# Linear attention with two channel mixes on one core: running sums ahead of the second tile's loads, last outputs in two column parts, fillers in planned TensorE gaps

## The chip, the cores and the metric

The kernel runs on one core of a Trainium2 chip. The metric is the device time of one execution in microseconds. Three timed executions of the kernel before took 407.04, 409.69 and 410.55 us, median 409.69. The profiled execution took 407.03 us; its profile spans 405.2 us, so 1.8 us lie outside the span.

## The reference, cut to what matters

```python
# attention: 4 batches x 8 heads, 768 steps, head size 32, state 16, in chunks
cum = np.cumsum(log_a_of_the_chunk)                  # running sums
L = np.exp(cum[:, None] - cum[None, :]) * causal
y = ((C @ B.T) * L) @ x  +  (C @ state) * np.exp(cum)
state = np.exp(sum(log_a)) * state + (B * decay_from_j).T @ x
# channel mix on the 3072 rows of 256 (x_prev is x one step earlier)
xk = mu_k * x + (1 - mu_k) * x_prev ; xr = mu_r * x + (1 - mu_r) * x_prev
k = np.maximum(xk @ w_k, 0)                          # 256 -> 1024
x = sigmoid(xr @ w_r) * ((k * k) @ w_v)              # w_r 256 -> 256, w_v 1024 -> 256
# second mix
h = np.maximum(np.maximum(x @ w1, x @ w2), x @ w3)   # 256 -> 768
out = h @ w_out                                      # 768 -> 256
```

The activations come as float32 and the weights as float64.

## The kernel before, in words

The 3072 rows are worked through in six tiles of 512 (t = 0 to 5). Each tile goes through attention, the gate (w_r, `gate`, matmuls on line L986), the first mix (`ffn`: eight blocks f of w_k on L1011, then w_v on L1032), `combine`, the maxout over w1, w2 and w3 (`maxout`, L689), and the projection by w_out (`project`, L1108, evacuated on L1079 by ScalarE and L1081 by VectorE).

To keep float32 precision every operand of the large products is split into a high and a low part (names that end in h and l), and each product is three matmuls: high x high, high x low, low x high. The high part is a copy (L414, mostly ScalarE), the low part a subtraction (L422, VectorE or GpSimd).

The float64 weights are fetched as pairs of 32-bit words into a buffer h (for w_k also woh) and made into float32 by five steps: ScalarE L630, then VectorE L631, L633, L635 and L637. After that they are split like the rest. In the order listings h_94 and h_93 are the two large fetch buffers, h_92 and wd or wol hold the words being converted. The first block of w_k for each of the two row halves (w_k0, into h, and w_k1, into woh) serves f = 0 to 3; the second half of w_k (into h_93, then wol, with low part wkl) serves f = 4 to 7.

Attention of tile 0: spreads (L703, L704) make the exponents of L, L860 the scores C times B, L872 on VectorE the product with L, L773 gathers the states (block c = 0 or 1), L895 multiplies by x, L885 adds what the state carries, and the copy L933 writes the result xb in two halves, one on ScalarE and one on VectorE. L966 and L968 mix it with the row before into tmp, which is split into k2h and k2l for the gate of tile 0. The running sums over the sequence (L600, L611; evacuated by L604 and by L605, an Exp) go out to DRAM as crd and ced and come back for the later tiles. For tile 1 the spread is on L719, L721 and L727; L727 is a burst of small matmuls.

All loads and stores are issued by SyncE in program order. The order of every engine's instructions is written by a planner, the class `Plan`: it simulates all operations with estimated durations, repeats the simulation with new priorities for `ROUNDS` times, and issues the operations by the start times of the best round. `first=` and `bias` shift priorities, `FETCH`, `HEAVY` and `OPEN` are its guesses for instruction fetch and DMA, `AHEAD` shifts the mix of tile 0 and the w_k conversions. Loads of tile 1 and the second half of w_k may not be issued before the operation in `begun['loads']` has ended; before the change that is L848, the product ce of tile 0. `Plan.issue` also puts a filler matmul (128x512, bfloat16) into a gap of the planned TensorE timeline if the gap is long enough, up to a time `stop`, the first planned start of a gate's matmul. `idle`, the end of the last TensorE operation there, is computed from its start and its estimated cost.

Of the kernel before, what the change touches and what calls it, by code (L numbers as in the profile page):

```python
# [11 lines left out]
AF = mybir.ActivationFunctionType  # L12
# [63 lines left out]
class Plan:  # L76
# [14 lines left out]
    FIRST = 1500.0  # L91
    STAY = 8000.0
    BLOCK, FRONT = 128, 92
    FETCH = ((9000.0, 5600.0), (16500.0, 2800.0), (30000.0, 5000.0), (60000.0, 3200.0), (1e9, 2600.0))
    OPEN = (1000.0, 28.0)
    HEAVY = (2100.0, 16000.0, 1300.0)
    WARM = (3400.0, 430.0, 215.0, 100.0, 600.0)
    EARLY = 104
    ROUNDS = 60
    SPARE = (200.0, 1000.0)  # L100
# [213 lines left out]
    def issue(self):  # L314
        ops, start, where = self.ops, self.start, self.where
        idle = 0.0
        stop = min(start[i] for i in self.wait_for)
        for i in sorted(range(len(ops)), key=lambda k: (start[k], k)):
            fn = ops[i][1]
            if where[i] == "PE":  # L320
                for _ in range(0 if idle else self.EARLY):
                    self.narrow()
                if self.WARM[0] < start[i] < stop:
                    gap = start[i] - max(idle, self.WARM[0]) - self.WARM[3 + (idle > 0.0)]
                    for _ in range(0 if start[self.switch[0]] < start[i] <= start[self.switch[1]] else int(gap / (self.WARM[1] if start[i] < self.COLD else self.WARM[2]))):
                        self.filler(idle > 0.0)
                idle = start[i] + ops[i][0]["PE"]
            if where[i]:
                fn(where[i]) if len(ops[i][0]) > 1 else fn()

# [6 lines left out]
SPREAD = 2  # L337
LATE = 0
EARLY1 = -20000.0
AHEAD = (60000.0, 60000.0)  # L340
FIRST = (9.85e5, 9.8e5, 9.9e5, 9.83e5, 9.5e5, 9.95e5, 9.6e5)


# [1 line left out]
def kernel(  # L345
# [56 lines left out]
    def act(n):  # L402
        return 93 + 0.833 * n

    def tt(n):
        return 68 + 1.042 * n
# [18 lines left out]
    def dma(cost, out_, in_, r=(), w=(), first=0.0, **k):  # L425
        plan.bias += first
        i = op("SP", 0.8 * cost, lambda: Q.dma_start(ap(out_), in_), r=r, w=w, **k)
        plan.bias -= first
        return i
# [167 lines left out]
    def sums():  # L597
        b_er.readers = [op("DVE", 130, lambda: V.tensor_copy(tri_r, tri_f), r=[b_cr], w=[b_tri], after=[begun['spread']])]
        p = boot.bufs[3]
        op("PE", 350, lambda p=p: [T.matmul(  # L600
            p.ap[:QH, s * P:(s + 1) * P], la[:, s * QH:(s + 1) * QH], tri, start=True, stop=True) for s in range(2)],
            r=[b_la, b_tri], w=[p])
        pr = p.ap[:QH, :2 * P].rearrange("r (s x) -> r s x", s=2)
        op("ACT", act(256), lambda: A.activation(crow[:, :, 0], pr, AF.Copy), r=[p], w=[b_cr])  # L604
        op("ACT", act(256), lambda: A.activation(crow[:, :, 1], pr, AF.Exp), r=[p], w=[b_er])  # L605
        for s in range(2):
            dma(200, ced[s * QH:(s + 1) * QH], crow[:, s, 1], r=[b_er], w=[b_ced[s]])
            dma(200, crd[:, s * QH:(s + 1) * QH].rearrange("c q i -> q c i"),
                crow[:, s, 0].rearrange("q (c i) -> q c i", c=2), r=[b_cr], w=[b_crd[s]], first=EARLY1)
        p = boot.bufs[2]  # L610
        op("PE", 350, lambda p=p: T.matmul(p.ap[:, :NC], tri, la, start=True, stop=True), r=[b_la, b_tri], w=[p])  # L611
        b_cc.readers = [k for s in (b_af, b_ts) for k in s.readers + s.writers]
        op("ACT", act(NC), lambda p=p: A.activation(ccol, p.ap[:, :NC], AF.Copy), r=[p], w=[b_cc])
# [179 lines left out]
    def attention(t):  # L793
# [49 lines left out]
        if not first:  # L843
# [3 lines left out]
        n = TW // (1 + c0)  # L847
        k = op({"DVE": tt(n), "POOL": pool(n)}, 0, lambda e: (V if e == "DVE" else G).tensor_mul(ov, cv, ev),  # L848
               r=[b_ct, b_ec], w=[b_ce], lock=True)
        begun.setdefault('loads', k)  # L850

        parts = 2 if first else 1
        step = NB // parts
# [84 lines left out]
    def three(w, xx):  # L938
        return [(w[0], xx[0]), (w[0], xx[1]), (w[1], xx[0])]
# [11 lines left out]
    def pe(cost, fn, r, w, after=()):  # L951
        return op("PE", cost, fn, r=r, w=w, after=after)
# [145 lines left out]
            rs.append(dma(step * 1.7, out[t, k, :, cols], o.ap[:, cols], r=[w]))  # L1098
        o.writers, o.readers = ws, rs

    def project(k, p, gs, after=()):
        cs = slice(k * P, (k + 1) * P)

        def go():
            for g in gs:
                terms = three([w[:, g, cs] for w in (wo_l[0](), wo_l[1]())], [h_t[g]()[:, s, :] for s in range(2)])
                for i, (l, r_) in enumerate(terms):
                    T.matmul(p.ap, l, r_, start=(g == 0 and i == 0), stop=(g == GC - 1 and i == 2))  # L1108

        pe(len(gs) * 3 * 227.3, go, [kk for g in gs for kk in b_h[g]] + [b_wo[k][g // 2] for g in gs], [p], after)  # L1110

    def final(t, k, after=()):
        p = pm.next()
# [1 line left out]
        finish(t, k, p, (("DVE", "ACT"),))  # L1115

    def final_last(t):
        for gs in (range(GC - 2), range(GC - 2, GC - 1), range(GC - 1, GC)):
            for k in range(KC):
                project(k, pc.bufs[2 * k], gs)  # L1120
                if GC - 1 in gs:
                    finish(t, k, pc.bufs[2 * k], (("ACT",), ("DVE",)))


    plan.bias = BIAS[0]
    attention(0)
    plan.switch = begun['spread'], begun['carried']
    plan.bias = 0.0
    weights_front()
    sums()  # L1130
    weights_back()
    for k in b_h[0]:
        for bb in (b_cr, b_er):
# [91 lines left out]
```

## Time and profile before

| what | value |
|---|---|
| timed executions | 407.04, 409.69, 410.55 us (median 409.69) |
| profiled execution | 407.03 us, span 405.2 us |
| TensorE | 395.2 us busy, 98% of the span |
| TensorE weight loads | 317.3 us |
| VectorE | 256.6 us |
| ScalarE | 215.8 us |
| GpSimd | 54.8 us |
| chain that ended last | TensorE 77%, VectorE 14%, DMA 5%, issue 2%, ScalarE 1% |

Busy times can overlap, weight loads with matmuls above all. The chain follows the work that ended last back from the last instruction, at each step to what released it. Idle time that is listed with a releaser is the time for which an instruction's engine stood still until that releaser ended.

### The profile page before, as it was taken

The numbers are of one execution on the slowest core, as the hardware profiler recorded it, in microseconds if no ns is written. First come the engines' busy times: TensorE is split into PE (matmuls) and PEld (weight loads), VectorE is DVE, ScalarE is ACT, GpSimd is POOL, SyncE is SP. The second block draws the span as 40 slices with busy tenths as digits, with TensorE's granted clock in tenths as the row PEclk, the third lists the DMA queues.
The fourth block names the chain that finished last, engine by engine and source line by source line (L and its number), as shares of the span: only waits on it lengthen the run. The fifth ranks groups of instructions, "written<-read, shape, count | busy, mean of one in ns | idle before, by whom it ended". The sixth has DMA issues, their size and how long they took to land.

```text
span 405.2 us, 8647 instructions
## 1 busy us (share of the span) xinstructions
PE 395.2 (98%) x3674; PEld 317.3 (78%) x3674; DVE 256.6 (63%) x417; ACT 215.8 (53%) x379; POOL 54.8 (14%) x60
## 2 busy tenths in 40 slices
PE   8879999999999999999999999999999999999996
PEld 5657877788887888888888887888787888888885
DVE  5789999999998944573735473745374315530632
ACT  6589879954767642355734255753256733321321
POOL 5211000000004100431400221320022200010010
PEclk9999999999999999999999999999999999999999
DMA  7595649541335100306000002200000000001001
GB/s 253 191 368 186 191 138 266 162 131 51 123 114 159 54 26 0 92 17 191 18 26 2 30 1 74 58 26 0 2 2 27 0 26 2 0 0 54 0 0 53
DMA packets 12879, 31.55 MB, mean 78 GB/s; under 512 B 1768, under 2 KB 4136, under 8 KB 12072
## 3 DMA queue, kind: packets, MB, share of 16 engines
q1 hardware_dynamic: 12840, 30.99, 24.4%
q8 instruction: 29, 0.48, 0.5%
q14 instruction: 10, 0.08, 0.1%
HBM read 27.64 MB, written 3.34 MB: 76 GB/s over the span
## 4 chain that ended last, share of the span: by engine, by line
PE 77%; DVE 14%; DMA 5%; issue 2%; ACT 1%; SPq 0%; ACTq 0%; DVEq 0%
PE pa L689 32%; PE pa L1032 14%; PE pa L1011 13%; PE pa L1108 9%; PE pa L986 3%; DMA h<-in_w_v_dram 3%; PE pb L1108 2%; DMA bt<-in_b_t_dram 2%; DVE L L872 1%; DVE tmp L1070 1%; PE pb L895 1%; PE pb L860 1%; DVE k2l L422 1%; DVE tmp L968 1%; DMA outs<-in_w_out_dram 1%
## 5 line engine op out<-in xcount | busy, mean ns | idle before, releaser
L1070 DVE TENSOR_TENSOR tmp<-tmp,pa 128x512 f32<-128x512 f32 x72 | 49.2, 687 | 55.6 <-PE pa L689 54.7
L422 DVE TENSOR_TENSOR k2l<-tmp,k2h 128x512 fp32r<-128x512 f32 x53 | 39.2, 750 | 41.8 <-ACT tmp L1020 33.9
L414 ACT ACTIVATE hr<-tmp 128x512 fp32r<-128x512 f32 x35 | 22.1, 632 | 69.4 <-DVE tmp L1070 69.2
L1032 PE MATMUL pa<-k2h,wvh 128*128 128x512 f32 x96 | 38.2, 398 | 0.0
L1032 PE MATMUL pa<-k2h,wvl 128*128 128x512 f32 x96 | 38.0, 395 | 0.0
L1032 PE MATMUL pa<-k2l,wvh 128*128 128x512 f32 x96 | 37.8, 393 | 0.0
L1108 PE MATMUL pa<-hr,worh 128*128 128x512 f32 x120 | 37.4, 393 | 0.0
L1017 ACT ACTIVATE tmp<-pa 128x512 f32<-128x512 f32 x48 | 28.3, 590 | 10.2 <-PE pa L1011 8.7
L1068 ACT ACTIVATE tmp<-pa 128x512 f32<-128x512 f32 x36 | 21.5, 596 | 21.8 <-PE pa L689 20.2
L1018 ACT ACTIVATE k2h<-tmp 128x512 fp32r<-128x512 f32 x48 | 30.2, 631 | 2.7 <-PE pa L1032 1.0
L422 DVE TENSOR_TENSOR hr<-tmp,hr 128x512 fp32r<-128x512 f32 x28 | 19.5, 700 | 14.8 <-ACT hr L414 14.7
L1108 PEld LDWEIGHTS pa<-hr,worh 128*128 128x128 f32 x120 | 22.3, 188 | 5.3 <-ACT th L991 0.7
L422 POOL TENSOR_TENSOR hr<-tmp,hr 128x512 fp32r<-128x512 f32 x8 | 10.3, 1293 | 111.0 <-ACT hr L414 111.0
L1020 ACT ACTIVATE tmp<-tmp 128x512 f32<-128x512 f32 x37 | 23.2, 631 | 0.8
L1108 PE MATMUL pa<-hr,worl 128*128 128x512 f32 x60 | 23.3, 389 | 0.0
L1032 PEld LDWEIGHTS pa<-k2h,wvh 128*128 128x128 f32 x96 | 18.0, 188 | 4.4 <-ACT k2h L414 0.2
L1032 PEld LDWEIGHTS pa<-k2h,wvl 128*128 128x128 f32 x96 | 18.0, 188 | 4.3
L1032 PEld LDWEIGHTS pa<-k2l,wvh 128*128 128x128 f32 x96 | 18.0, 188 | 4.1
L790 POOL TENSOR_TENSOR sbd<-sbd,um 128x256 f32<-128x256 f32 x2 | 3.1, 1546 | 117.0 <-DVE sbd L788 117.0
L1079 ACT ACTIVATE outs<-pa 128x512 f32<-128x512 f32 x9 | 5.4, 599 | 25.3 <-PE pa L1108 25.3
L968 DVE SCALAR_TENSOR_TENSOR tmp<-xb,bits,tmp 128x512 f32<-128x512 f32 x24 | 17.2, 747 | 0.4
L872 DVE TENSOR_TENSOR L<-pb,L 128x512 f32<-128x512 f32 (+1 forms) x28 | 15.7, 607 | 2.1 <-PE pb L860 1.3
(273 smaller groups left out, 975.1 us busy)
## 6 DMA issues: line engine op xcount, KB each, us to landing
h<-in_w_dram SPq DMA_DIRECT2D x6, 768.0 KB, 4.7
L<-crd SPq DMA_DIRECT2D x8, 512.0 KB, 6.8
cw<-in_c_w_dram SPq DMA_DIRECT2D x6, 512.0 KB, 5.2
xt<-in_x_l_dram SPq DMA_DIRECT2D x6, 512.0 KB, 7.9
out_dram<-outs SPq DMA_DIRECT2D x10, 256.0 KB, 2.1
h<-in_w_v_dram SPq DMA_DIRECT2D x2, 1024.0 KB, 7.7
bt<-in_b_t_dram SPq DMA_DIRECT2D x6, 256.0 KB, 5.0
bl<-in_b_l_dram SPq DMA_DIRECT2D x6, 256.0 KB, 6.9
```

The costliest lines, as they stand in the source:

```text
L414: A.activation(ap(out_), ap(in_), AF.Copy)
L422: op({"DVE": tt(n), "POOL": pool(n, narrow)}, 0, lambda e: (V if e == "DVE" else G).tensor_sub(ap(out_), ap(x0), ap(x1)), r=r, w=w, after= ...
L689: T.matmul(pt, l, r_, start=(i == 0), stop=(i == last))
L968: op("DVE", 61 + tt(n), lambda tv=tv, c=c: V.scalar_tensor_tensor(out=tv, in0=xb[:, c, bs, :P], scalar=om[:, i, c:c + 1], in1=tv, op0=ALU. ...
L1011: T.matmul(p.ap[:, :n], l, r_, start=(c == 0 and i == 0), stop=(c == KC - 1 and i == 2))
L1017: op("ACT", 51 + 0.833 * n, lambda: A.activation(sq, p.ap[:, :n], AF.Relu), r=[p], w=[tm])
L1018: op("ACT", act(n), lambda: A.activation(hi, sq, AF.Square), r=[tm], w=[kb])
L1020: A.activation(sq, sq, AF.Square) if e == "ACT" else
L1032: T.matmul(pv[c2].ap[:, :n], l, r_, start=(f == 0 and i == 0), stop=(f == FC - 1 and i == 2))
L1068: op("ACT", 51 + 0.833 * TW, lambda p=p, tm=tm: A.activation(tm.ap, p.ap, AF.Copy), r=[p], w=[tm])
L1070: op("DVE", tt(TW), lambda p=p, tm=tm: V.tensor_tensor(out=tm.ap, in0=tm.ap, in1=p.ap, op=ALU.max), r=[p], w=[tm])
L1108: T.matmul(p.ap, l, r_, start=(g == 0 and i == 0), stop=(g == GC - 1 and i == 2))
```

## The change

The change has four parts.

1. In `sums`, the Exp of the running sums (L605) becomes `begun['loads']`, the stores of ced get a priority, and `sums()` is declared ahead of `weights_front()`. The loads of tile 1 and of the second half of w_k therefore wait for the Exp of the sums and no longer for ce.
2. Numbers of the planner: one limit and one duration in `FETCH`, `AHEAD` from 60000 to 40000.
3. Fillers: the slack that a gap must have beyond the fillers falls from 600 to 200 ns, the first gate's start is included, and `idle` is the planned end of the last operation (with its planned instruction fetch) and no longer start plus cost.
4. The last tile's outputs: for each 128 output columns k the 512 rows are projected in two parts of 256, each into a PSUM bank of its own; ScalarE evacuates the first part and VectorE the second, each followed by a store of 128 KB. Before, one bank of 512 was projected and its two halves were evacuated.

```diff
-    FETCH = ((9000.0, 5600.0), (16500.0, 2800.0), (30000.0, 5000.0), (60000.0, 3200.0), (1e9, 2600.0))
+    FETCH = ((9000.0, 5600.0), (19000.0, 2800.0), (30000.0, 4500.0), (60000.0, 3200.0), (1e9, 2600.0))
-    WARM = (3400.0, 430.0, 215.0, 100.0, 600.0)
+    WARM = (3400.0, 430.0, 215.0, 100.0, 200.0)
...
-                if self.WARM[0] < start[i] < stop:
+                if self.WARM[0] < start[i] <= stop:
...
-                idle = start[i] + ops[i][0]["PE"]
+                idle = self.ends[i]
...
-AHEAD = (60000.0, 60000.0)
+AHEAD = (40000.0, 40000.0)
...
-        op("ACT", act(256), lambda: A.activation(crow[:, :, 1], pr, AF.Exp), r=[p], w=[b_er])
+        begun['loads'] = op("ACT", act(256), lambda: A.activation(crow[:, :, 1], pr, AF.Exp), r=[p], w=[b_er])
         for s in range(2):
-            dma(200, ced[s * QH:(s + 1) * QH], crow[:, s, 1], r=[b_er], w=[b_ced[s]])
+            dma(200, ced[s * QH:(s + 1) * QH], crow[:, s, 1], r=[b_er], w=[b_ced[s]], first=FIRST[4] - 2e5)
...
-        begun.setdefault('loads', k)
...
-    def project(k, p, gs, after=()):
+    def project(k, p, gs, after=(), xs=slice(0, TW)):
...
-                terms = three([w[:, g, cs] for w in (wo_l[0](), wo_l[1]())], [h_t[g]()[:, s, :] for s in range(2)])
+                terms = three([w[:, g, cs] for w in (wo_l[0](), wo_l[1]())], [h_t[g]()[:, s, xs] for s in range(2)])
                 for i, (l, r_) in enumerate(terms):
-                    T.matmul(p.ap, l, r_, start=(g == 0 and i == 0), stop=(g == GC - 1 and i == 2))
+                    T.matmul(p.ap[:, :xs.stop - xs.start], l, r_, start=(g == 0 and i == 0), stop=(g == GC - 1 and i == 2))
...
     def final_last(t):
+        o = [outr.next() for _ in range(KC)]
+        base = [k.readers + k.writers for k in o]
         for gs in (range(GC - 2), range(GC - 2, GC - 1), range(GC - 1, GC)):
             for k in range(KC):
-                project(k, pc.bufs[2 * k], gs)
-                if GC - 1 in gs:
-                    finish(t, k, pc.bufs[2 * k], (("ACT",), ("DVE",)))
+                for s in range(2):
+                    p, xs = pc.bufs[2 * k + s], slice(s * HW, (s + 1) * HW)
+                    project(k, p, gs, xs=xs)
+                    if GC - 1 in gs:
+                        w = Buf()
...
+                        op("DVE" if s else "ACT", tt(HW) if s else act(HW), run, r=[p], w=[w], after=base[k])
+                        dma(HW * 1.7, out[t, k, :, xs], o[k].ap[:, xs], r=[w])
...
     plan.bias = 0.0
+    sums()
     weights_front()
-    sums()
```

The planner turns this into another order on every engine. Three places matter here. The first is SyncE's queue at the start of the program, as a difference (minus before, plus after).

```order
 L427 DMA la<-in_a_l_dram 128x224
 L427 DMA bits<-in_mus_dram 128x4
-L427 DMA h_94<-in_w_k_dram 128x1024
 L427 DMA cw<-in_c_w_dram 128x1024
 L427 DMA bt<-in_b_t_dram 128x512
```

One row further on (bl) it goes on:

```order
 L427 DMA h_94<-in_w_r_dram 128x1024
 L427 DMA xt_121<-in_x_l_dram 128x1024
+L427 DMA h_94<-in_w_k_dram 128x1024
 L427 DMA ct<-in_c_t_dram 128x512
 L427 DMA woh<-in_w_k_dram 128x1024
 L427 DMA ct<-in_c_t_dram 128x512
+L427 DMA xt_121<-in_x_l_dram 128x1024
+L427 DMA h_94<-in_w_v_dram 128x2048
+L427 DMA ced<-h_91 96x128 x2
 L427 DMA h_93<-in_w_k_dram 128x2x1024
 L427 DMA bl<-in_b_l_dram 128x512
```

The first block of w_k, third in the queue before, is now eighth, behind the loads of tile 0. Further down, the second half of w_k (h_93) and bl of tile 1 stood directly behind ct of tile 1; now the load of x for tile 2, the first half of w_v and the two stores of ced come ahead of them.

The second place is ScalarE between the end of tile 0's attention and the gate. Before:

```order
L966 ACTIVATE tmp_107<-xb_129,bits 128x512
L966 ACTIVATE tmp_109<-xb_129,bits 128x512
L966 ACTIVATE tmp_110<-xb_129,bits 128x512
L414 ACTIVATE wkh<-wd 128x512
L630 ACTIVATE wol<-h_93 128x1024
L414 ACTIVATE k2h_99<-tmp_107 128x512
L414 ACTIVATE k2h_101<-tmp_108 128x512
```

After:

```order
L605 ACTIVATE h_91<-pa_134 96x2x128
L965 ACTIVATE tmp_107<-xb_129,bits 128x512
L965 ACTIVATE tmp_109<-xb_129,bits 128x512
L965 ACTIVATE tmp_110<-xb_129,bits 128x512
L414 ACTIVATE k2h_99<-tmp_107 128x512
L613 ACTIVATE ccol<-pa_133 128x192
L414 ACTIVATE k2h_101<-tmp_108 128x512
```

The first k2h stood behind two steps of w_k; now it follows the mix directly, and the Exp of the sums (L605) is ahead of the mix. L630 on h_93 comes later, behind both Tanh of the gate and L630 of w_v.

The third place is TensorE between the spread of tile 1 and the gate of tile 0 (L985 after the change is L986 before). Before:

```order
L721 MATMUL pb_135<-lal,tri 128x512
L727 MATMUL pb_135<-tri,la 64x64 x32
L986 MATMUL pa_131<-k2h_99,wrh 128x512
L986 MATMUL pa_131<-k2l_100,wrh 128x512
L986 MATMUL pa_131<-k2h_99,wrl 128x512
```

After:

```order
L727 MATMUL pb_135<-tri,la 64x64 x32
L1181 LDWEIGHTS identb
L1181 MATMUL pa_131<-identb 128x512
L1181 LDWEIGHTS identb
L1181 MATMUL pa_131<-identb 128x512
L1181 LDWEIGHTS identb
L1181 MATMUL pa_131<-identb 128x512
L1181 LDWEIGHTS identb
L1181 MATMUL pa_131<-identb 128x512
L985 MATMUL pa_131<-k2h_99,wrh 128x512
```

Four fillers stand between the burst and the gate. Two more are ahead of the spread, and one that stood between two spreads of tile 0 is gone. The spread of the other half of tile 1, which stood behind the first block of w_k (f = 0), now stands ahead of it.

## Rows read from the trace of the kernel before

**Rows 1.** Waits of TensorE: what waited, for what, us in total, times, longest.
```profile
PE pa L986 <- ACT k2h L414: 1.3, 1, 1.3
PE pb L719 <- DVE xb L933: 0.8, 1, 0.8
PE pa L1011 <- DVE outs L1081: 0.3, 1, 0.3
```

**Rows 2.** Stretches: length; busy PE, PEld, DVE, ACT, POOL (count); clock, DMA share, GB/s.
```profile
5.00:10.00 5.00, 4.78 (x28) 2.01 (x34) 3.92 (x11) 3.54 (x8) 1.48 (x5) 1.00 1.01 388
...
60.00:80.00 20.00, 19.22 (x98) 15.11 (x104) 20.00 (x33) 18.86 (x34) 0.00 (x0) 1.00 0.76 208
...
100.00:120.00 20.00, 20.00 (x387) 16.08 (x386) 19.71 (x43) 14.29 (x31) 0.00 (x0) 1.00 0.36 112
...
140.00:160.00 20.00, 20.00 (x89) 16.37 (x88) 10.78 (x17) 8.80 (x15) 0.00 (x0) 1.00 0.03 13
```

**Rows 3.** The chain that ended last: start us, us, what; pieces of it.
```profile
2.65 6.96 DMA bt<-in_b_t_dram
...
19.09 10.50 DMA h<-in_w_v_dram
...
37.01 1.19 DVE wkl L422
...
61.56 0.61 DVE xk00l L422
...
96.62 0.69 DVE bd L764
...
124.12 0.70 DVE outs L1081
...
396.28 5.45 PE pb L1108 x24
```

**Rows 4.** SyncE's DMA issues in order of time: start, us of issuing, what.
```profile
1.70 0.43 SPq L427 DMA_DIRECT2D h<-in_w_k_dram  x1
...
16.37 0.43 SPq L427 DMA_DIRECT2D h<-in_w_k_dram  x1
```

**Rows 5.** ScalarE ahead of the gate; in brackets the idle time before, and its releaser.
```profile
19.88 1.95 ACT L966 ACTIVATE tmp<-xb,bits 128x512 f32<-128x512 f32 x3
...
23.26 1.13 ACT L630 ACTIVATE wol<-h 128x1024 f32<-128x1024 f32 x1 [0.91 <-DMA h<-in_w_k_dram]
24.28 1.14 ACT L414 ACTIVATE k2h<-tmp 128x512 fp32r<-128x512 f32 x2
```

**Rows 6.** VectorE, same columns, 18 to 30 us.
```profile
18.56 0.69 DVE L635 SCALAR_TENSOR_TENSOR wd<-woh,wd 128x512 uint32<-128x512 uint32 x1
19.16 0.69 DVE L933 COPY xb<-pb 128x512 f32<-128x512 f32 x1
...
24.94 1.35 DVE L422 TENSOR_TENSOR k2l<-tmp,k2h 128x512 fp32r<-128x512 f32 x2 [1.35 <-ACT k2h L414]
...
29.01 0.68 DVE L631 TENSOR_SCALAR wol<-wol 128x1024 f32<-128x1024 f32 x1
```

**Rows 7.** TensorE ahead of the gate, same columns.
```profile
23.19 0.46 PE L727 MATMUL pb<-tri,la 64*64 64x64 f32 x15 [0.92 <-issue]
24.95 0.50 PE L986 MATMUL pa<-k2h,wrh 128*128 128x512 f32 x1 [1.31 <-ACT k2h L414]
```

**Rows 8.** The last evacuations and stores, same columns.
```profile
400.81 2.17 SPq L427 DMA_DIRECT2D out_dram<-outs  x4
...
401.75 0.38 ACT L1079 ACTIVATE outs<-pb 128x256 f32<-128x256 f32 x1 [0.98 <-PE pb L1108]
402.17 0.42 DVE L1081 TENSOR_SCALAR outs<-pb 128x256 f32<-128x256 f32 x1 [0.93 <-ACT outs L1079]
```

**Rows 9.** Weight loads of w_out's products (page, part 5: busy, mean ns, idle before).
```profile
L1108 PEld LDWEIGHTS pa<-hr,worh 128*128 128x128 f32 x120 | 22.3, 188 | 5.3 <-ACT th L991 0.7
```

**Rows 10.** L592 alone (eight loads, eight 64-column matmuls): stretch, busy PE, PEld, clock.
```profile
12.16:13.06 0.90, 0.89 (x8) 0.89 (x8) 1.00 0.35 141
```

More of the change, by code (lines that the diff above doesn't have):

```diff
@@ L1105, in go @@
             for g in gs:
-                terms = three([w[:, g, cs] for w in (wo_l[0](), wo_l[1]())], [h_t[g]()[:, s, :] for s in range(2)])
+                terms = three([w[:, g, cs] for w in (wo_l[0](), wo_l[1]())], [h_t[g]()[:, s, xs] for s in range(2)])
                 for i, (l, r_) in enumerate(terms):
-                    T.matmul(p.ap, l, r_, start=(g == 0 and i == 0), stop=(g == GC - 1 and i == 2))
-        pe(len(gs) * 3 * 227.3, go, [kk for g in gs for kk in b_h[g]] + [b_wo[k][g // 2] for g in gs], [p], after)
+                    T.matmul(p.ap[:, :xs.stop - xs.start], l, r_, start=(g == 0 and i == 0), stop=(g == GC - 1 and i == 2))
+        pe(len(gs) * 3 * 0.444 * (xs.stop - xs.start), go, [kk for g in gs for kk in b_h[g]] + [b_wo[k][g // 2] for g in gs], [p], after)
     def final(t, k, after=()):
@@ L1117, in final_last, with run @@
     def final_last(t):
+        o = [outr.next() for _ in range(KC)]
+        base = [k.readers + k.writers for k in o]
         for gs in (range(GC - 2), range(GC - 2, GC - 1), range(GC - 1, GC)):
             for k in range(KC):
-                project(k, pc.bufs[2 * k], gs)
-                if GC - 1 in gs:
-                    finish(t, k, pc.bufs[2 * k], (("ACT",), ("DVE",)))
+                for s in range(2):
[3 more added lines that the diff above has]
+                        w = Buf()
+                        def run(o=o[k], p=p, xs=xs, s=s):
+                            if s:
+                                V.tensor_scalar(out=o.ap[:, xs], in0=p.ap[:, :HW], scalar1=0.5, scalar2=None, op0=ALU.mult)
+                            else:
+                                A.activation(o.ap[:, xs], p.ap[:, :HW], AF.Copy, scale=0.5)
+                        op("DVE" if s else "ACT", tt(HW) if s else act(HW), run, r=[p], w=[w], after=base[k])
+                        dma(HW * 1.7, out[t, k, :, xs], o[k].ap[:, xs], r=[w])
     plan.bias = BIAS[0]
```

## The prediction, written before the changed kernel ran

> **What bounds the kernel now.** I read the busy table first: TensorE is busy for 395.2 of 405.2 us, so only two things can shorten the run: its idle time and the work before its first and after its last matmul. Then the list of what TensorE waited for [rows 1]. The reader is to see that the waits are few and single ones: 1.3 us for k2h ahead of the gate of tile 0, 0.8 us for the copy L933, 0.3 us for an output's evacuation (L1081). Third, the busy times by stretch [rows 2]: from 60 to 120 us VectorE has no time left (20.00 of 20 us, later 19.71), from 140 us on it is half idle (10.78 of 20). Fourth, the chain that ended last [rows 3]. It runs through loads of tile 0, then through VectorE (conversion of the second half of w_k, then xk00l at 61.56), and touches VectorE for the last time at 124.12 (L1081); from there TensorE alone carries it to the last outputs. So time won before 124 us counts only as far as VectorE wins it too, and what is won there is kept to the end.
>
> **Base.** All durations are from the profiled execution, 407.03 us = span 405.2 + 1.8 outside. It is close to the lowest timed run (407.04); the median 409.69 is 2.66 above it, and no row says why. I sum against 407.03 and come back to this.
>
> **Change 1, the start.** The 512 KB of w_k0 leave the place ahead of tile 0's loads [rows 4]. The DMA engines were full there at 388 GB/s [rows 2], so these bytes are worth 1.35 us to the loads behind them, and the issue slot 0.47. bt, in flight for 6.96 us [rows 3], lands between 0 and 1.8 us earlier. By itself this reaches TensorE only if the copy of tile 0's result does too: L933 on VectorE started at 19.16, behind L635 on w_k1 [rows 6], and TensorE waited 0.8 us for it [rows 1]. With w_k0 converted later in VectorE's order than w_r, the copy comes earlier, and the spread of tile 1 starts earlier by between 0.8 (the wait alone) and 1.8 (the whole lead of bt). I take 0.8, because the work between the two is not shortened. Two fillers ahead of that spread lie in the same wait; at 5.45/24 = 0.227 us for 512 columns [rows 3] they cost 0.45 if it is gone.
>
> **The gate.** k2h started at 24.28, directly behind L630 on the second half of w_k, which had waited 0.91 us for its DMA [rows 5]. L966 had been through at 19.88 + 1.95 = 21.83. With both w_k steps moved behind, k2h can start 2.45 us earlier, less one ScalarE evacuation that comes in ahead (L605, by the 0.38 us of another 256 columns [rows 8]): 2.1 us. TensorE has a second condition: the burst L727 ended at 23.19 + 0.46 = 23.65, after a stop of 0.92 that no engine caused [rows 7]. It moves by the 0.8 above, and four fillers follow, 4 x 0.227 = 0.91: 23.76 if that stop stays, 22.84 if it goes, against 24.95 before. So the gate starts 1.2 to 2.1 us earlier; I take 1.5. In all, five more fillers (seven for two) are 1.1 us of TensorE work, and all of it lies in the waits just costed.
>
> **From the gate to 62 us.** The chain here is VectorE's. It had stood still for 1.35 us ahead of k2l [rows 6]; this idle time can now be worked. What it loses: bd of tile 1, formerly on GpSimd, at 0.69 [rows 3]. Its lead at xk00l is then between 1.35 - 0.69 = 0.7 and the gate's 1.5. I take 1.1.
>
> **From 62 to 124 us.** VectorE is full [rows 2], so the lead does not grow. There it is between nothing (if other rows come over to VectorE) and 2.1 + 0.3, since the buffer for which TensorE waited at 124 [rows 1, 3] is now freed by ScalarE. I take **1.0**, near the 1.1 at 62 us.
>
> **Change 2, planner numbers.** They act by the orders costed above and add no work.
>
> **Change 3, the last outputs.** Before, VectorE's half came behind ScalarE's: 401.75 + 0.38, then 402.17 + 0.42 [rows 8]. Now the last two matmul groups are ScalarE's halves, VectorE's are done before, and the last evacuation is one of 0.38. That takes 0.42 us off the end. SyncE issues four stores as before [rows 8]. The price: 36 matmuls of 512 columns become 72 of 256, each with a load of 128 columns. By the columns a matmul is 0.227/2 = 0.1135 us. A load of 128 columns with a matmul of only 64 went every 0.90/8 = 0.112 us [rows 10]; so load and 256 columns just fit, and I take 0. The other end is the load's busy time of 188 ns [rows 9] in every step: 72 x (0.188 - 0.1135) = +5.4 us. I take the near row because its loads have the same 128 columns.
>
> The Trainium skill, page "TensorE: Matmul & The Clock Gate", section "Part 3: Packing small matmuls — row/col tiling", speaks against this edit: it says that a weight load overlaps with running matmuls only if they use other row groups. The rows here disagree for 512 columns, since 188 ns of load per 227 ns would leave too little for the columns. By that rule the 36 additional loads would all stand in the open, +3.0 us by the price worked out under the rivals.
>
> **Sum:** -1.0 - 0.4 = -1.4: **405.6 us** on the scale of the profiled execution. Of three timed runs two were 2.7 and 3.5 us higher; I expect the same scatter and put a third of 2.66 on top: **406.5 us**.
>
> **Rivals.**
>
> *VectorE gives the lead back* (25%). For: it is full from 60 to 120 [rows 2], and rows that GpSimd had come to it. Then the gate starts earlier and TensorE waits later, at 62 and 124. Left is the end's 0.42: 406.6, with the scatter 407.5.
>
> *The fillers eat the waits* (5%): the planned gaps are not the real ones and the change does not do what it says. The copy comes no earlier, the gate starts at 23.65 + 0.91 = 24.56, and VectorE's 0.69 takes the rest: again 406.6.
>
> *All of the lead stays* (10%): 2.1 + 0.3 + 0.42 = 2.8: 404.2. For: after 124 us nothing waits. Against: VectorE.
>
> *The second half of w_k comes too late* (19%), **slower**. Its issue was at 16.37 [rows 4] and its landing let L630 start at 23.26 [rows 5], 6.9 us later. Now it is queued behind the ced stores, which wait for L605, and L605 stands just ahead of the L966 that started at 19.88: issue at about 20. Ahead of it 1 MB of w_v is in flight, whose transfer took 10.50 us [rows 3]. So it lands between 20 + 6.9 = 26.9 and 20 + 10.5 = 30.5. VectorE's first step on it began at 29.01 [rows 6], and L630 needs 1.13 before: a landing up to 27.9 costs nothing, and from there on wkl at 37.01 [rows 3] and all behind it slide, by up to 2.6. With the end's 0.42: up to 409.2, with the scatter 410.1. Against: VectorE can convert w_v in that time.
>
> *The halves are bound by weight loads* (6%), **slower**. L592's step of 0.112 holds 64 columns worth 0.227/8 = 0.028, so the load's share is at most 0.084. If it doesn't hide behind 256 columns, 36 more loads cost 36 x 0.084 = +3.0: 408.6; by the 188 ns, +5.4: 411.0. It decides from a step above 0.1135 on.
>
> **How the numbers follow.** My forecast has 35%. The range reaches from 403.6 (the whole lead, and a little less at the start) to 410.0: a high draw of the timed runs on my forecast gives 405.6 + 3.5 = 409.1, on the cases of no gain 406.6 + 3.5 = 410.1, and late w_k 409.2 to 410.1. What can be told from no change is about 1%, 4.1 us: the three runs alone spread over 3.5. Below that bound lies only the full lead together with a low draw, 10%. Above it lie the loads at 188 ns, and the late w_k with a high draw, 12%. In between 78%.
>
> **What would show it.** In the profile of the changed kernel: bt's flight shorter; the wait for L933 gone from TensorE's list; k2h directly behind the mix and the gate's first matmul between 22.8 and 23.8; VectorE busy from there without the 1.35 us gap; L630 on the second half of w_k without a DMA wait longer than 0.9, wkl ending before 38.2; at 62 us TensorE ahead by about 1.1; no wait at 124; at the end matmuls of 256 columns every 0.113 us and one evacuation behind the last. I am wrong if VectorE shows new idle time between 24 and 40 us, if the last 72 matmuls take more than 8.5 us, or if TensorE waits again for VectorE between 62 and 124 by as much as it led.

## The result

The changed kernel is slower: 413.8 us median of 6 executions (411.41 to 415.25) against 409.36 (407.04 to 410.55) for the kernel before, a ratio of 1.0128 with a 95% interval of 1.010 to 1.0157. A second series beside another set of experiments (e0 below) gave 413.0 against 408.51, ratio 1.0099 (1.0068 to 1.013). Forecast were 406.5 us and a range up to 410.0. One of the six executions of e3 below was in a slower state and is left out of its numbers.

The profiled execution took 415.25 us, span 413.5. The first view is the list of what TensorE waited for (who waits, for whom, us in total, times, longest), to be held against [rows 1]. "issue" means that the profile shows nothing that was waited for.

```profile
PE pa L1010 <- ACT tmp L1016: 2.4, 3, 1.4
PE pb L894 <- issue: 2.0, 2, 1.8
PE pb L719 <- DVE xb L932: 1.7, 1, 1.7
PE pa L1031 <- DVE k2l L422: 1.7, 2, 1.1
...
PE pb L773 <- DMA xt<-in_x_l_dram: 1.0, 1, 1.0
...
PE pb L1107 <- DVE outs L1129: 0.2, 1, 0.2
```

The wait of the gate for k2h (1.3 us before) is gone, and so is that on L1081 at 124 us. In their place stand others. Three of them were there before and are longer now: the copy (L932, before L933) 1.7 for 0.8, the blocks of w_k behind ScalarE (L1010, before L1011) 2.4 for 0.8, and the stop without a releaser in the bursts L894 (before L895) 2.0 for 0.2. The rest is new. Next, TensorE from the gate on and at the burst L894 of tile 2:

```profile
20.58 0.38 PE L719 MATMUL pb<-future,identb 128*128 128x512 bf16 x1 [1.68 <-DVE xb L932]
...
23.07 1.04 PE L1181 MATMUL pa<-identb 128*128 128x512 bf16 x4
23.76 0.58 PE L985 MATMUL pa<-k2h,wrh 128*128 128x512 f32 x1
...
111.42 0.72 PE L894 MATMUL pb<-L,xt 64*32 64x64 f32 x48 [1.77 <-issue]
```

The gate starts at 23.76 us, 1.19 earlier than in [rows 7]. So the change does what it says at the place it aims at. The stretches (as in [rows 2]) show where it is lost:

```profile
30.00:35.00 5.00, 4.03 (x79) 3.08 (x78) 3.37 (x6) 3.94 (x7) 0.00 (x0) 1.00 0.94 330
60.00:80.00 20.00, 18.60 (x81) 14.80 (x81) 16.16 (x26) 14.84 (x28) 0.00 (x0) 1.00 0.74 184
...
100.00:120.00 20.00, 18.23 (x322) 14.98 (x321) 19.82 (x39) 12.00 (x24) 0.00 (x0) 1.00 0.27 92
```

From 60 to 80 us VectorE, the full engine of this stretch, works 16.16 us where it worked 20.00 [rows 2]. Near 30 us it stood still for the load of bl, which is issued behind the second half of w_k; near 79 us for a ScalarE step that waited for a DMA. VectorE's and ScalarE's rows for it, in brackets the idle time and its releaser:

```profile
31.63 0.69 DVE L764 TENSOR_TENSOR bd<-bl,dfj 128x512 f32<-128x512 f32 x1 [2.58 <-DMA bl<-in_b_l_dram]
32.24 0.69 DVE L631 TENSOR_SCALAR wol<-wol 128x1024 f32<-128x1024 f32 x1
...
79.15 0.56 DVE L631 TENSOR_SCALAR wd<-wd 128x768 f32<-128x768 f32 x1 [2.81 <-ACT wd L630]
```

```profile
31.00 1.13 ACT L630 ACTIVATE wol<-h 128x1024 f32<-128x1024 f32 x1 [1.81 <-DMA h<-in_w_k_dram]
...
78.21 0.91 ACT L630 ACTIVATE wd<-h 128x768 f32<-128x768 f32 x1 [2.63 <-DMA h<-in_w_dram]
```

The two loads and what was ahead of them in SyncE's queue (to be compared with [rows 4]):

```profile
20.00 0.33 SPq L427 DMA_DIRECT2D h<-in_w_v_dram  x1
...
21.73 0.43 SPq L427 DMA_DIRECT2D h<-in_w_k_dram  x1
...
67.82 0.63 SPq L427 DMA_DIRECT2D ec<-ced  x1
68.73 15.48 SPq L427 DMA_DIRECT2D h<-in_w_dram  x3
```

The second half of w_k is issued 5.4 us later than before. And at 67.82 the load of ec for tile 2 (it is filled from ced) stands ahead of a load of w1 to w3, which the text calls the w load from here on. In the kernel before the w load came first, and ScalarE's step on it started 4.7 us after its issue, without a wait:

```profile
66.03 0.38 SPq L427 DMA_DIRECT2D h<-in_w_dram  x1
67.40 0.63 SPq L427 DMA_DIRECT2D ec<-ced  x1
```

```profile
70.73 0.90 ACT L630 ACTIVATE wd<-h 128x768 f32<-128x768 f32 x1
```

In the changed kernel it is 9.5 us, from 68.73 to 78.21. This swap lies 22 DMA issues behind the stores of ced, which the edit names.

As a sum over the two profiled executions: the gate of tile 0 is 1.2 us early; the first w_v matmul of f=4 (53.22 us before) is 3.5 us late; the gate of tile 1 (82.40) 4.6 late, with the scores of tile 2 (1.1 us) still to do; the gate of tile 2 (114.85) 8.3 late, 1.8 of it from the stop at L894. The wait at 124 us, now gone, gives 0.4 back, the last outputs take 0.4: 8.3 in the span.

### The profile page after: what moved, and what is told of

The parts are those of the page before. It is cut to its first block, busy times and chain, and to the rows that moved or that the text cites. A ratio compares the mean times of both kernels' runs of the same rounds, so it can differ in the third digit from the quotient of the medians.

```text
span 413.5 us, 8727 instructions
## 1 busy us (share of the span) xinstructions
PE 398.1 (96%) x3715; PEld 319.4 (77%) x3715; DVE 258.3 (62%) x419; ACT 215.3 (52%) x378; POOL 50.6 (12%) x58
## 4 chain that ended last, share of the span: by engine, by line
PE 79%; DVE 9%; DMA 8%; issue 2%; ACT 1%; SPq 1%; DVEq 0%; ACTq 0%
PE pa L689 35%; PE pa L1031 12%; PE pa L1010 11%; PE pa L1107 10%; DMA bl<-in_b_l_dram 4%; PE pa L985 3%; DMA h<-in_w_dram 2%; PE pb L1107 2%; PE pb L894 2%; DMA h<-in_w_v_dram 2%; PE pb L884 1%; PE pb L859 1%; PE pb L773 1%; DVE L L871 1%; SPq L427 1%
## 5 line engine op out<-in xcount | busy, mean ns | idle before, releaser
L422 DVE TENSOR_TENSOR hr<-tmp,hr 128x512 fp32r<-128x512 f32 x28 | 19.2, 691 | 14.8 <-ACT hr L414 14.7
```

Source lines behind the costliest of these rows:

```text
L422: op({"DVE": tt(n), "POOL": pool(n, narrow)}, 0, lambda e: (V if e == "DVE" else G).tensor_sub(ap(out_), ap(x0), ap(x1)), r=r, w=w, after= ...
```

## The experiments

All ratios are to the kernel before, run on the same chip beside the experiment, with 95% intervals. In the kernels that "move" one instruction the planner's result is kept and only that instruction's place in the order of its engine is changed; L numbers shift by a few lines there.

| run | what | median us (before) | ratio (interval) |
|---|---|---|---|
| e0 | changed kernel again | 413.0 (408.51) | 1.0099 (1.0068 to 1.013) |
| e1 | before + last outputs in parts | 409.48 (408.75) | 1.0015 (0.9989 to 1.004) |
| e2 | before + fillers | 408.28 (408.75) | 0.999 (0.9966 to 1.0015) |
| e3 | before + edit of the loads' release | 413.39 (408.75) | 1.0102 (1.0052 to 1.0153) |
| e4 | changed, five loads ahead | 416.4 (408.75) | 1.0184 (1.0142 to 1.0227) |
| e5 | changed, two loads ahead | 412.69 (408.76) | 1.009 (1.0063 to 1.0117) |
| e6 | changed without the loads' edit | 411.32 (408.76) | 1.0049 (1.0022 to 1.0077) |
| e7 | changed, burst later | 413.5 (408.76) | 1.0106 (1.0068 to 1.0144) |
| e8 | before, k2h ahead of L630 | 407.56 (408.76) | 0.9971 (0.9944 to 0.9998) |
| e9 | changed, ec behind the w load | 410.0 (408.51) | 1.0048 (1.0026 to 1.0069) |
| e10 | changed, e5 + e7 + e9 | 411.04 (408.51) | 1.0066 (1.0044 to 1.0089) |
| e11 | e8 + fillers | 408.25 (408.51) | 1.0004 (0.9986 to 1.0022) |
| e12 | before, ec ahead of the w load | 410.32 (408.56) | 1.0056 (1.0032 to 1.0079) |
| e13 | changed, e5 + e9 | 410.35 (408.56) | 1.0047 (1.003 to 1.0064) |
| e14 | e8 again | 407.71 (408.56) | 0.9984 (0.9964 to 1.0004) |

### The parts alone: e1, e2, e3, e6

**e1** takes the edit of `project` and `final_last` only:

```diff
-                project(k, pc.bufs[2 * k], gs)
+                for s in range(2):
+                    p, xs = pc.bufs[2 * k + s], slice(s * HW, (s + 1) * HW)
+                    project(k, p, gs, xs=xs)
```

> The kernel before with the last outputs in two column parts and nothing else changed. In the profile of the changed kernel the 72 small matmuls go every 0.120 us (8.64 us against 36 x 0.2268 = 8.16), TensorE waits 0.32 us for a VectorE evacuation of the same PSUM tile, and the span ends 0.5 us sooner after the last matmul. If these three are all, this kernel is +0.2 to +0.4 us against the one before (same). Rival: the tail carries a good part of the 4 to 5 us; then +2 or more.

Its chain of the last 10 us:

```profile
393.15 7.21 PE pb L1108 x60
...
400.39 0.44 DVE outs L1130
...
400.87 1.35 PE pb L1108 x9
...
402.23 0.38 ACT outs L1132
```

7.21/60 = 0.120 us per matmul of 256 columns, against 0.1135 for half of 512 [rows 3]: 72 x 0.0065 = 0.5 us. TensorE moreover waits 0.2 us for VectorE's evacuation although that reads another bank. In the code both banks of one k are halves of one tile; that the order is kept by tile is read from there and was not tested. Against this stands the one evacuation less [rows 8]. From the gate of tile 5 to the end both profiles with the new tail, this one and the changed kernel's, take 0.4 us more than the kernel before (102.8 for 102.4). The medians say +0.7 us, not told from nothing; the tail doesn't carry the loss, nor does it bring the 0.42.

**e2** takes the new rule for fillers only.

```diff
-                if self.WARM[0] < start[i] < stop:
+                if self.WARM[0] < start[i] <= stop:
-                idle = start[i] + ops[i][0]["PE"]
+                idle = self.ends[i]
```

> The kernel before with the new rule for fillers alone; every other engine's order is as before. If fillers lie in real waits, 0 to +0.3 us. Rival: they delay the gate and everything behind it through VectorE's full stretch, +0.5 to +1.5 us, and the gate starts later than 24.95.

In its profile nine fillers stand ahead of the gate, and the gate starts at 26.34, later than 24.95:

```profile
24.58 2.12 PE L1169 MATMUL pa<-identb 128*128 128x512 bf16 x9
26.34 0.58 PE L986 MATMUL pa<-k2h,wrh 128*128 128x512 f32 x1
```

TensorE's granted clock was at 1.2 GHz from 15.6 to 22.5 us in this execution, so the late gate is not the fillers' work alone. The first w_v matmul of f=4 is 1.0 us later there, and the execution took 1.1 us more than the profiled one before (408.09 for 407.03). The medians don't show it: 408.28 for 408.75. So fillers cost nothing that the medians can tell. Six of the 12 executions had the full clock (a mean granted clock of 0.998 or more), 22 of 101 of the kernel before; among these the means are 408.0 and 407.3 us, so a cost that the clock gives back is possible and was not tested.

**e3** takes only the edit of the loads' release.

```diff
-        op("ACT", act(256), lambda: A.activation(crow[:, :, 1], pr, AF.Exp), r=[p], w=[b_er])
+        begun['loads'] = op("ACT", act(256), lambda: A.activation(crow[:, :, 1], pr, AF.Exp), r=[p], w=[b_er])
-        begun.setdefault('loads', k)
```

> The kernel before with only the edit of the loads' release (Exp of the running sums instead of ce, priority of the ced stores, sums ahead of the weights); the planner then writes another order for all engines. If the late loads of the second tile and of the second half of w_k are the cause, this kernel is +3 to +5 us, with a wait of L630 for the second half of w_k of more than 1.5 us and VectorE idle for more than 2 us near 29 us. Rival: the loss comes with the planner's other numbers (AHEAD); then within 1 us of before.

+4.6 us by the medians, +4.2 by the ratio: this edit alone brings as much as the whole change, within the noise. ScalarE's wait is there,

```profile
31.07 1.12 ACT L630 ACTIVATE wol<-h 128x1024 f32<-128x1024 f32 x1 [1.88 <-DMA h<-in_w_k_dram]
```

and the first w_v matmul of f=4 is 5.4 us late. The order that the planner writes here is not that of the changed kernel, though: ec (60.00 us) stands far from the w load (71.81).

**e6** is the complement, the change without that edit.

```diff
+        begun.setdefault('loads', k)
-    sums()
     weights_front()
+    sums()
```

> The changed kernel with the edit of the loads' release undone; planner numbers, fillers and the two column parts stay. With e3 this splits the change in two. If e3's edit carries the loss, this one is within 1 us of before, and TensorE has no stop of its own (issue) after 26 us. Rival: AHEAD adds its own loss; +2 or more.

+0.5%, 2.0 us by the ratio: not within 1 us of before, so the rival with AHEAD holds in part; how much of it is AHEAD, the tail (e1) or the fillers was not taken apart. e3 and e6 together make 1.5%, more than the change, but within e3's interval. Each of them makes the planner write a new order, so they need not add up. Here the gate starts at 22.83, the stop on L895 is 0.7 us at most, and TensorE waits for the low part of the second half of w_k:

```profile
40.01 0.79 PE L1011 MATMUL pa<-xk00h,wkl 128*128 128x512 f32 x1 [2.50 <-DVE wkl L422]
40.60 0.63 PE L1011 MATMUL pa<-xk01h,wkh 128*128 128x512 f32 x1
41.03 0.63 PE L1011 MATMUL pa<-xk01l,wkh 128*128 128x512 f32 x1
```

### The late loads: e4, e5

**e4** moves the second half of w_k, bl, x, bt and cw of tile 1 directly behind ct of tile 1.

```diff
+    for n, i in enumerate(sorted(begun['moved'], key=lambda i: plan.start[i])):
+        plan.start[i] = plan.start[begun['ct1']] + 0.001 * (n + 1)
```

> The changed kernel with all orders held, but SyncE issues the second half of w_k, then bl, x, bt and cw of tile 1 directly behind ct of tile 1 as before, ahead of x of tile 2, of w_v and of the ced stores. If their late issue (21.7 us instead of 16.4) is the cause, L630 on the second half starts at 28 to 29 instead of 31.0, VectorE's idle time of 2.6 us near 29 goes, the first w_v matmul of f=4 is 2.5 to 3.5 us earlier, and the time is +1 to +2.5 us against before instead of +4 to +5. Rival (VectorE's own new order makes it late whatever the loads do): still +4 to +5 us, with VectorE's idle time replaced by another wait.

It got worse, 1.0184. w_v is now the late one, and ScalarE's L630 on w_v is ahead of L630 on w_k in its order:

```profile
32.36 1.12 ACT L630 ACTIVATE h<-h 128x1024 f32<-128x1024 f32 x1 [4.95 <-DMA h<-in_w_v_dram]
```

So the test did not take the lateness away, it moved it. **e5** moves only the first two:

```diff
+    for n, i in enumerate((begun['half2'], begun['bl1'])):
+        plan.start[i] = plan.start[begun['ct1']] + 0.001 * (n + 1)
```

> The changed kernel with all orders held but for two loads: the second half of w_k and bl of tile 1 are issued directly behind ct of tile 1, in the time when the DMA engines have little to do (15 to 20 us); w_v keeps its place as the next large load. In e4 w_v landed late instead and ScalarE stood 4.95 us before its L630. If the late start of the stream of loads is the cause, L630 on the second half waits for no DMA, VectorE's 2.6 us of idle time near 29 us shrinks to under 1.3 us, VectorE's first step on wol starts at 30 to 31 us instead of 32.24, and the time is 1.5 to 2.5 us under the changed kernel's 413.8, so +2 to +3.5 against before. Rival (bandwidth: w_v then lands later by what the others gain): as late as before, +4 to +6.

```profile
30.29 0.69 DVE L631 TENSOR_SCALAR wol<-wol 128x1024 f32<-128x1024 f32 x1 [1.05 <-ACT wol L630]
```

VectorE's step on w_k starts 1.95 us earlier than in the changed kernel, as foreseen, and in the profile the first w_v matmul of f=4 is back at 53.34. But the median falls by only 1.1 us, and the interval overlaps those of both series of the changed kernel. From 60 to 80 us VectorE still has only 17.30 of 20 us.

**e0**, the changed kernel unaltered, shows why.

> The changed kernel itself, unaltered, beside the others on the same chip: +4 to +6 us against before; stop of TensorE on L894 near 109 us of 1.5 to 2 us, wait of L630 for the second half of w_k of 1 to 2 us, and VectorE idle for 2 us or more between 60 and 80 us, if these are features of the order and not of one execution.

```profile
28.86 0.69 DVE L764 TENSOR_TENSOR bd<-bl,dfj 128x512 f32<-128x512 f32 x1 [0.65 <-DMA bl<-in_b_l_dram]
...
76.97 0.56 DVE L631 TENSOR_SCALAR wd<-wd 128x768 f32<-128x768 f32 x1 [4.83 <-ACT wd L630]
```

In this execution the loads near 30 us were hardly late (0.65 us of idle time for 2.58). VectorE's step on w_k started at 29.47, earlier than in e5, and the first w_v matmul of f=4 came 0.55 us ahead of the kernel before. So what e5's profile shows near 30 us, the unaltered kernel can show too. The time was lost between 60 and 80 us instead: 4.83 us of idle time for 2.81. Two executions of one kernel lose at different places; what they share is the wait for the w load and the stop at L894 (1.69 us here).

### The order of two DMA issues: e9, e12

**e9** puts the load of ec for tile 2 behind the next w load, one row later in SyncE's queue.

```diff
+    move(begun['ec2'], plan.start[sp_[sp_.index(begun['ec2']) + 1]] + 0.001)
```

> The changed kernel with one DMA issue moved: the load of ec for tile 2 comes behind the next load of w1 to w3 in SyncE's queue, as it stood before. In the changed kernel SyncE waited with ec until 67.8 us, the load behind it landed at 78.1, and VectorE stood 2.8 us for L630 on it. If this head of the queue is a cause of its own, VectorE's idle time between 60 and 80 us (3.8 us) falls to about 1, TensorE's two waits for k2l at 82 to 85 us (2.0 us) go, and the time is 1 to 2 us under the changed kernel run beside it. Rival: the wait is only the late conversion handed on; no change.

2.1 us less by the ratios, 3.0 by the medians, against e0 run beside it. Its rows of SyncE, ScalarE and VectorE, then those of SyncE and ScalarE in e0:

```profile
65.77 0.38 SPq L427 DMA_DIRECT2D h<-in_w_dram  x1
66.19 0.63 SPq L427 DMA_DIRECT2D ec<-ced  x1
```

```profile
71.95 0.91 ACT L630 ACTIVATE wd<-h 128x768 f32<-128x768 f32 x1 [0.71 <-DMA h<-in_w_dram]
```

```profile
72.89 0.56 DVE L631 TENSOR_SCALAR wd<-wd 128x768 f32<-128x768 f32 x1 [0.64 <-ACT wd L630]
```

```profile
64.40 0.63 SPq L427 DMA_DIRECT2D ec<-ced  x1
65.31 16.73 SPq L427 DMA_DIRECT2D h<-in_w_dram  x3
```

```profile
76.04 0.89 ACT L630 ACTIVATE wd<-h 128x768 f32<-128x768 f32 x1 [4.67 <-DMA h<-in_w_dram]
```

The w load is issued at 65.3 in e0 and at 65.8 in e9. With ec ahead of it the step that waits for it started at 76.04, 10.7 us after the issue; with ec behind it at 71.95, 6.2 us after. In this order it is not SyncE's time that is lost but the place in the transfers. VectorE then has 19.36 us of work in 60 to 80, and TensorE no wait for k2l.

**e12** is the test from the other side, in the kernel before.

```diff
+    move(sp_[sp_.index(begun['ec2']) - 1], plan.start[begun['ec2']] + 0.001)
```

> The kernel before with one DMA issue moved, all else held: the load of w1 to w3 that SyncE issued at 66.03 us comes behind the load of ec of tile 2 (67.40), as in the changed kernel. If this order alone costs what e9 gave back, L630 on that load (70.73 before) starts at 74 to 76, VectorE stands 2 to 4 us between 70 and 78 us, and the time is +1.5 to +3 us. Rival (it costs only where VectorE is late already): VectorE has other work, under +0.7.

```profile
68.74 0.63 SPq L427 DMA_DIRECT2D ec<-ced  x1
69.48 11.38 SPq L427 DMA_DIRECT2D h<-in_w_dram  x3
```

```profile
74.66 0.89 ACT L630 ACTIVATE wd<-h 128x768 f32<-128x768 f32 x1 [1.72 <-DMA h<-in_w_dram]
```

+0.56%, 2.3 us by the ratio, 1.8 by the medians: one swap of two DMA issues, with nothing else changed, costs about half of the whole loss. In the profile TensorE was 1.3 us behind the kernel before at the first w_v matmul of f=4 (its granted clock was at 1.2 GHz from 25.2 to 28.7 us) and 3.7 at the gate of tile 2. Of the 2.4 between, 0.8 came ahead of the step that the swap delays, and 1.6 lie behind it.

The way is another one here than in e9. The step started only 5.2 us after the issue of the w load, near the 4.7 us of the kernel before, but the issue came late: ec stood at the head of SyncE's queue until 68.74 waiting for a VectorE step, while the buffer of the w load had been free since 67.30 (the end of L637), so that it was issued at 69.48 for 66.03. So the two runs show that the order of these two issues costs some 2 us in either kernel, and that it does so in two ways: by the transfers in the changed kernel, by the queue in the kernel before.

### The stop at the burst, and the repairs together: e7, e10, e13

**e7** moves the burst L894 of tile 2 behind two groups of the maxout.

```diff
+    move(pe_[n + 1], at)
+    move(pe_[n + 2], at + 0.1)
+    move(begun['y2'], at + 0.2)
```

> The changed kernel with one TensorE operation moved: the burst L894 of tile 2 (128 small matmuls), which follows the 128 small ones of L773 and L884 directly, comes behind two groups of the maxout (2.7 us of large matmuls). In the changed kernel TensorE stopped there for 1.8 us with no releaser; e3 and e4 show the same, before and e1 none. If the stop comes from bursts in a row, it is gone or under 0.5 us and the time falls by 1.2 to 1.8 us, to +3 against before. Rival: the stop stays whatever lies ahead, or a wait for VectorE takes its place; then no change against the changed kernel.

The stop is gone (the 0.3 us in the list is one in tile 0, at 14.7 us), but waits stand in its place, which the changed kernel did not have:

```profile
PE pa L689 <- ACT tmp L1070: 0.6, 1, 0.6
...
PE pa L1013 <- ACT outs L1081: 0.5, 1, 0.5
PE pb L894 <- issue: 0.3, 1, 0.3
...
PE pa L689 <- DVE tmp L1072: 0.3, 1, 0.3
```

The interval overlaps the changed kernel's, so what the stop costs net stays open. What it is can be read from the traces. In the 17 profiles together TensorE stands still 31 times for more than 0.15 us without a releaser, and only at four places of its own program, counted in its recorded instructions, weight loads and matmuls above all, from the start: at the 707th, the 962nd, the 1987th and the 3011th, within one. The stop at L727 [rows 7] is at the second. The distances are multiples of 256, within one. The changed kernel's TensorE has 7451 instructions on record, and the queue that carries instructions brings 29 blocks of 16 KB (29 x 256 = 7424). TensorE passes these places 68 times in the 17 profiles. It stopped in all 29 passes in which the last block had started up to 2.2 us before it came there, and in 2 of the 39 in which the block had started earlier. At the 3011th these are 0.5 us in the changed kernel (109.15 for 109.65), 3.8 in the kernel before and 4.4 in e7. All this fits one cause: TensorE waits for the next block of its program. L773 and L884, 128 small matmuls with as many loads, are 256 instructions and passed in 1.9 us, so behind them the block comes too late, and behind e7's large matmuls it does not.

**e10** has all three moves of e5, e7 and e9 (their diffs together).

> The changed kernel with the three moves of e5 (two loads ahead), e7 (burst L894 later) and e9 (ec behind the w load) together, all else held. If these are the three causes, the sum of e5's 1.1 to 3.8, e7's 0.3 to 1.6 and e9's 1 to 2 brings it to within 2 us of before (0 to +2). Rival (VectorE's order or its added work is a fourth cause): +2.5 to +4 remains.

+2.5 us by the medians: a miss, and no better than e9 alone. **e13** leaves the burst out (the diffs of e5 and e9).

> The changed kernel with e5's and e9's moves in SyncE's queue and no other. e9 alone was at 1.0048 of before. If the late second half of w_k is a cause beside it, 0.5 to 1.5 us under e9, so 0 to +1.5 us against before. Rival (once ec is behind, VectorE catches up by itself): as e9, +1.5 to +2.5.

As e9. Once ec is behind, two loads ahead bring nothing more that can be told. What remains, some 1.9 us by the ratio, is the size of the tail (e1) and the stop at L894 (1.3 us in its profile) together; that they are the cause was not shown apart. Ten of its 11 executions had the full clock, with a mean of 410.3 us for 407.3 of the kernel before at full clock, so at the same clock 3.0 us remain, and about 1 us of that has no cause yet.

### The lead of the gate: e8, e14, e11

**e8** changes one place in the kernel before: both k2h come ahead of L630 on the second half of w_k.

```diff
+    move(begun['half2'] + 1, plan.start[begun['mix'] + 6] + 0.001)
```

> The kernel before with one ScalarE instruction moved: L630 on the second half of w_k comes behind both k2h, not ahead of them. All else is held. The gate should start near 23.7 (the end of the burst) instead of 24.95 and VectorE's idle time of 1.35 us ahead of k2l shrink. If a lead of the gate lives through VectorE's full stretch (the forecast), the time is 0.7 to 1.3 us under before; if VectorE gives it back, 0 to 0.3.

**e14** is the same kernel in another series.

> e8's kernel (the one before with k2h ahead of L630) once more, beside the others, since e11 did not repeat its gain. If the gain is real, 0.995 to 0.999 of before; if it was one chip's share of executions at the full clock, 0.999 to 1.001.

```profile
22.86 0.46 PE L729 MATMUL pb<-tri,la 64*64 64x64 f32 x15 [0.63 <-issue]
23.25 0.50 PE L990 MATMUL pa<-k2h,wrh 128*128 128x512 f32 x1
```

In e14 the gate starts 1.7 us early; by the first w_v matmul of f=4 0.45 is left of it, and nothing at the gate of tile 1 (82.36 us for 82.40; 82.39 in e8). 0.9971 and 0.9984 in two series, the second interval reaching to 1.0004: about 0.2% under the kernel before, and the lowest medians of all kernels here. But this is not the lead. 21 of the 24 executions of this kernel had the full clock, and 22 of 101 of the kernel before; among these the means are 407.6 and 407.3 us. What is gained is that more executions keep the clock. That the shorter wait ahead of the gate does this fits e12's profile, where the clock fell at 25.2 us, right behind that wait, but was not tested. **e11** adds the fillers to it.

> The kernel before with e8's one move (k2h ahead of L630) and the changed kernel's rule for fillers. e8 was at 0.997 of before and e2 at 0.999; both had more executions at the full granted clock than before. If the two add, 0.995 to 0.998 of before, and faster than both kernels. Rival: fillers take the same idle time that e8 fills; then as e8 alone.

1.0004: the two don't add; the gain of e8 is at the edge of what can be told.

## Why the prediction was wrong

**The start of tile 0** was half right. The scores of tile 0 began at 7.83 for 9.74, so bt's lead was there in full. The step to the copy failed: it was taken to come 0.8 us earlier and came at 19.85 for 19.16 (19.01 in e0). VectorE's order after the change has three steps of w_k0 and w_k1 between 16.70 and 19.93 ahead of the copy. I had read that w_k0 is converted later than w_r, and not where this puts it. Two of the three were slow besides: L635 took 1.76 us and L631 0.94 while GpSimd worked (16.42 to 19.04), for 0.69 and 0.42 earlier in the same trace (11.82 and 14.66) while it stood still. No row had priced that.

**The gate** was right in its number: 23.76 in a forecast window of 22.8 to 23.8, and 1.2 us of lead, the lower bound. k2h did come directly behind the mix. But the time of the other condition, the burst, was luck: it started 0.7 us later and not 0.8 earlier, and the stop of 0.92 us in it, which the late end of the window kept, was gone.

**From the gate to 62 us** was taken as +1.1 of lead. It was 3.5 us of loss in one profile and 0.5 of lead in the other (e0). Where nothing but the gate moves (e8, e14), 0.8 and 1.7 us at the gate were 0.4 at 53 us: the rival "VectorE gives the lead back" (25%) had this right, though not the loss. The rival of the late second half of w_k had the mechanism, with 19%. Its price was cut short: the issue came at 21.73 and not at 20, because L605 stands behind a ScalarE copy of w_k0 that waits for VectorE's L637 (19.93). By e5 its weight in the time is 1 us or less, not told from nothing, and by e13 nothing that can be told once the next step is mended.

**From 62 to 124 us** is the step that failed: "VectorE is full, so the lead does not grow", with 1.0 kept. In place of 1.0 us gained, TensorE lost 4.8 us between the first w_v matmul of f=4 and the gate of tile 2 in one profile (3.5 late, then 8.3) and 6.5 in e0 (0.55 early, then 6.0 late). I read the fullness of VectorE as a property of the stretch. It is one of the order of loads: a full engine that waits for one load in its queue loses all that time, and nothing gives it back. The sentence held the bound upward, and "if other rows come over to VectorE" was the only way down. The order of SyncE's queue past 35 us I had not costed, though the planner rewrote it there too. e9 and e12 show some 2 us for it by the ratios (1.8 to 3.0 by the medians), the largest single cause found. The second loss of this stretch, the stop at the burst, was in no rival; a stop of the same kind stood in [rows 7], and where the next one would fall was not asked. It comes where TensorE uses up a block of its program faster than the next arrives (e7).

**The last outputs** were taken as -0.42 and are about +0.4 to +0.7. The near row was right in kind: loads hide behind 256 columns but for 6.5 ns each, and the 188 ns are not borne out. What the sum lacked are these 6.5 ns per matmul and the wait for VectorE's evacuation. The rule of the Trainium skill that the prediction held against the edit (page "TensorE: Matmul & The Clock Gate", section "Part 3: Packing small matmuls — row/col tiling"), that a weight load overlaps with running matmuls only if they use other row groups, is not borne out by e1 either, with 0.120 us for a load and 256 columns.

**The fillers** cost nothing that the medians can tell, as taken (e2).

**The base**: the profiled execution before was one of the few at the full clock throughout (below), so adding a third of the gap to the median was too little. With the whole gap the forecast would have been 408.3 us, so this is not what made it wrong.

## What to carry to other kernels

Where a planner writes the order, a small edit at the start rewrites the queues of the whole program; read every engine's order to the end, the DMA issues above all, before a lead is carried forward. A lead ahead of a full engine is worth what that engine wins: 1.7 us at the gate (e14) were 0.45 us some 30 us later and nothing some 60 us later. A load that a full engine needs next should not stand behind one that is needed later: here it cost some 2 us. And before a small difference of medians is called a gain of the order, compare executions of the same granted clock.

## What the runs showed of the hardware

A load of 768 KB took longer to be used when a load of 256 KB (ec, the same row of DRAM written to 16 partitions) was issued just ahead of it. From its issue to the step that needed it passed 8.4 to 10.7 us with ec just ahead (the changed kernel, e0, e4, e5, e7) and 6.2 to 7.1 us with ec just behind (e9, e10, e13). Two loads of 512 KB (crd), issued just before, were still in flight in these runs (in e0 the later one landed at 70.06, the w load having been issued at 65.31). In e12, where it landed 0.8 us after the issue of the w load, it was 5.2 us even with ec ahead. So ec ahead is not enough by itself; what slows the transfers is open.

TensorE stopped without a releaser in the trace 31 times in 17 profiles, for 0.2 to 1.8 us, in bursts of small matmuls and only at places that lie multiples of 256 instructions apart (e7 above). That it waits for the next 16 KB of its program there is inferred from these transfers: each stop began 0.5 to 2.7 us after one had started.

TensorE's granted clock fell back from 2.4 to 1.2 GHz for 3.4 us or twice that in the middle of 7 of the 17 profiles. In e0 one such fall came behind 2.9 us in which TensorE was busy for 0.61 us (waiting for k2l); length, busy times and clock as in the stretches above:

```profile
78.00:80.90 2.90, 0.61 (x2) 0.30 (x3) 2.90 (x5) 2.87 (x6) 0.00 (x0) 1.00 0.00 0
80.90:84.30 3.40, 3.40 (x8) 2.26 (x9) 3.40 (x6) 3.34 (x7) 0.00 (x0) 0.50 0.46 60
```

The rows of e6 above show the same at 40.60 to 41.03: one matmul of 512 columns per 0.43 us for 0.227. Of 101 executions of the kernel before, 22 had the full clock (mean 407.3 us) and 79 had not (408.9). These 1.6 us are the larger part of the 2.66 us between its profiled execution and its median, which no row of its trace explained. That the falls alone make the difference is not shown.
